# Output weights by head group through a DRAM scratch, an epsilon column, whole-bank gate products and earlier transposes in a linear-attention and gated-MLP block

## The chip, the cores and the metric

The kernel runs on one core of one Trainium2 chip. The metric is the device time of one execution in microseconds (us); the median of three runs of the kernel before is 190.47 us (190.45 to 190.97). A core has a matrix engine (PE, whose weight loads the profile lists as PEld), a vector engine (DVE), a scalar engine (ACT), a GpSimd engine (POOL) and a sync engine (SP). Each works through its own list of instructions in order and waits for the others on semaphores. In this kernel SP and ACT issue the DMAs; the profile calls SP's queue q1 and ACT's q10. ps is the PE's result memory, eight banks of 512 f32 per partition.

## The reference

Two stages, 2048 tokens, width 448, 16 heads of 28, hidden width 1792; inputs and output are bf16.

```python
qkv = (x @ wqkv).reshape(B, S, 3, H, Dh)          # x is layer-normed
phi = lambda t: jnp.where(t > 0, t + 1, jnp.exp(t)) + 1e-6
pq, pk = phi(q), phi(k)
kv = jnp.einsum("bhsd,bhse->bhde", pk, v)
z = jnp.einsum("bhsd->bhd", pk)
num = jnp.einsum("bhqd,bhde->bhqe", pq, kv)
den = jnp.einsum("bhqd,bhd->bhq", pq, z)[..., None] + 1e-6
h = x + (num / den).reshape(B, S, D) @ wo
# then, on layernorm(h):
h2 = h + (_gelu(h_n @ w_gate) * (h_n @ w_up)) @ w_down
```

## The kernel before

The tokens are 16 tiles of 128 (t = 0 to 15) and 8 pairs of tiles (p = 0 to 7). Everything stays on the chip between the load of x and the store of the result.

**Keys and queries.** Each tile is normalized, transposed and multiplied by the key or query weights, four matmuls of 448 columns into one of ps banks 0 to 3 (tasks `k_t`, `q_t`, function `proj`, L469). ACT reads a query bank twice, `eq_t` (exp, L496) and `rq_t` (relu, L497), and only then is the bank free for the query tile four places later. Key tiles add to sums in banks 4 to 7 (`pt`, L488). So the v projection is never made per token: when all key tiles are in, the sums are copied to SBUF (`evpA`, `evpD`, L516 to L521), multiplied by wv into the per-head matrix kv (`kv`, L527), masked to its diagonal blocks (`kvm`, L531), and multiplied by wo to the output weights w2 (`w2_c`, L547), seven matmuls because the 448 rows are cut in 128-row pieces and the head groups are 112 rows wide. w2 is copied out of ps (`evwA`, `evwD`), and two DMAs (`dws0`, `dws1`, on SP's queue) make a copy w2s with the two halves of the partitions exchanged.

**Attention output of a pair** (`a2_pair`). pq is finished (`cq`, `aq`), multiplied by z (`t1`), summed per head (`dr`, L572 or L586), 1e-6 is added on ACT (`deA`, `deP`, L574 and L588), inverted (`rd`) and multiplied in (`pn`, into pqn). Pair 0 is transposed on the PE (`tro`); pairs 1 to 7 by a DMA on SP's queue (`oT_p`, L605). The product with w2 is 4 matmuls per tile for pair 0 (`out1_t`, L617), and for the others 14 matmuls of 64 rows, two at a time on the two halves of the array, in two parts (`outA_p`, `outB_p`, L627 and L628), of which B waits for A's results. Then follow the residual (`hr`), the second layer norm and the transpose of hn, on the PE for pair 0 (`trh`, L654), by DMA for the rest (`hT`).

**MLP.** Gate and up products go to the two halves of the array, into two alternating gate banks (0, 1) and up banks (6, 7) (`gu`, L731 and L733). ACT applies gelu (`ge`, L751), DVE multiplies by the up product (`hm`, L753), both in halves of 256 columns. The first four tiles are worked two at a time (14 units `gu2_0` to `gu2_13` of two hidden blocks), the rest four at a time (`gu4`). The down product is L697 and, for the last two tiles, L678.

**Order.** The tasks are recorded in program order, each with the buffers it reads and writes. The table ORDERS then gives for each engine the order of its tasks as a list of task numbers, and the semaphore waits are derived from the buffers. HOLD names for some tasks which of several waits comes first. The MLP weights are loaded by SP behind the DMA transposes of the x tiles, four loads of 672 KB (first 768 hidden columns) and 896 KB (the rest), gate and up each into 64 partitions; the last is the up load of 896 KB.

Of the kernel before, what the change touches and what calls it, by code (L numbers as in the profile page):

```python
# [822 lines left out]
```

## Time and profile before

| what | value |
|---|---|
| median of 3 runs | 190.47 us |
| profiled execution, first to last instruction | 188.3 us |
| PE busy | 184.3 us (98%) |
| PEld busy | 109.2 us (58%) |
| DVE busy | 129.3 us (69%) |
| ACT busy | 76.5 us (41%) |
| POOL busy | 50.0 us (27%) |
| granted PE clock | 1.000 over the whole span |
| DMA | 17.11 MB, of it 16.32 MB on q1 and 0.52 MB on q10 |

The span is 2.2 us shorter than the median of the runs; what lies around it (launch and end) is taken as unchanged. A line of a timeline is: start, duration, engine, source line, operation, what is written from what, how many, and in brackets the engine's idle time before it. Durations of neighbours overlap, since an engine starts the next instruction before the last has left its pipeline; the step from start to start is what counts. Durations of matmuls are modelled ends.

### The profile page before, as it was taken

Reading aid. Unit: us, or ns where it says so; the run is one execution under the profiler, and the core shown is the slowest. Engines: PE = TensorE matmul, PEld = TensorE weight load, DVE = VectorE, ACT = ScalarE, POOL = GpSimd, SP = SyncE. Lnnn points to the kernel's source line nnn. Section 1 sums busy time; section 2 is a strip of 40 time slices with the busy share of each in tenths; the row PEclk is TensorE's granted clock in tenths of the full one; section 3 lists DMA queues with packets and bytes.
Section 4 is the critical chain, followed back from the end, with each engine's and each line's share of the span. In section 5 each row is a group of like instructions: output and inputs, shape, how many; then the busy total and the mean of one; then the engine's idle time right before and its main releaser. Section 6 shows DMA issues by size and latency. Waiting matters only on the chain.

```text
span 188.3 us, 4459 instructions
## 1 busy us (share of the span) xinstructions
PE 184.3 (98%) x1813; PEld 109.2 (58%) x1813; DVE 129.3 (69%) x330; ACT 76.5 (41%) x220; POOL 50.0 (27%) x91
## 2 busy tenths in 40 slices
PE   7999999999999999999999999999999999999994
PEld 7545555555688788965554555555545545454554
DVE  4999959999899998786796762562645244335432
ACT  3878752799963231432234222321242222224100
POOL 6067910704505686033614000206100000000000
PEclk9999999999999999999999999999999999999999
DMA  5996458999393526820005720000096000002024
GB/s 169 387 231 88 96 104 194 218 222 174 65 320 64 95 52 116 84 52 0 0 3 98 144 54 0 0 3 2 3 135 111 3 0 24 3 0 98 3 79 140
DMA packets 35076, 17.11 MB, mean 91 GB/s; under 512 B 26864, under 2 KB 33648, under 8 KB 35056
## 3 DMA queue, kind: packets, MB, share of 16 engines
q1 hardware_dynamic: 34432, 16.32, 41.1%
q10 hardware_dynamic: 624, 0.52, 0.8%
q8 instruction: 14, 0.23, 0.5%
q14 instruction: 6, 0.05, 0.1%
HBM read 8.26 MB, written 1.84 MB: 54 GB/s over the span
## 4 chain that ended last, share of the span: by engine, by line
PE 94%; DVE 3%; DMA 1%; issue 0%
PE ps L733 38%; PE ps L697 19%; PE ps L469 12%; PE ps L731 9%; PE ps L488 6%; PE ps L627 3%; PE ps L678 3%; PE ps L628 2%; DMA x_sb<-in_A_x_dram 1%; DVE st L413 1%; PE ps L617 1%; PE ps L547 1%; PE ps L527 1%; PE ps L443 0%; PE ps L654 0%; DVE den L572 0%
## 5 line engine op out<-in xcount | busy, mean ns | idle before, releaser
L733 PE MATMUL ps<-hnT,wgu_sb 64*128 64x512 bf16 (+1 forms) x490 | 88.8, 333 | 0.0
L731 PE MATMUL ps<-hnT,wgu_sb 64*128 64x512 bf16 (+1 forms) x490 | 88.6, 333 | 0.0
L751 ACT ACTIVATE gl<-ps 128x256 bf16<-128x256 f32 x112 | 36.6, 383 | 85.3 <-PE ps L731 84.4
L753 DVE TENSOR_TENSOR hh<-ps,gl 128x256 bf16<-128x256 f32 x112 | 42.1, 416 | 41.4 <-ACT gl L751 41.3
L733 PEld LDWEIGHTS ps<-hnT,wgu_sb 64*128 64x128 bf16 x490 | 45.2, 94 | 32.9 <-DVE hh L753 3.4
L731 PEld LDWEIGHTS ps<-hnT,wgu_sb 64*128 64x128 bf16 x490 | 45.4, 94 | 2.5
L697 PE MATMUL ps<-wd_sb,hh 64*128 64x448 bf16 x392 | 41.5, 349 | 0.0
L697 PEld LDWEIGHTS ps<-wd_sb,hh 64*128 64x128 bf16 x392 | 23.2, 94 | 14.5
L469 PE MATMUL ps<-wqk_sb,xnT 128*128 128x448 bf16 x128 | 27.4, 353 | 0.0
L413 DVE BATCH_NORM_STATS2 st<-x_sb 128x6 f32<-128x448 bf16 x32 | 19.2, 612 | 1.8 <-DMA x_sb<-in_A_x_dram 1.7
L585 POOL TENSOR_TENSOR t<-pq,zbc 128x448 f32<-128x448 bf16 x12 | 12.3, 1042 | 23.7 <-DVE pq L583 22.0
L469 PEld LDWEIGHTS ps<-wqk_sb,xnT 128*128 128x128 bf16 x128 | 11.9, 98 | 11.4 <-DVE pk L482 0.8
L488 PE MATMUL ps<-pk,xnn 128*128 128x448 bf16 x64 | 13.9, 352 | 0.0
L627 PE MATMUL ps<-w,pqnT 64*128 64x448 bf16 x49 | 11.5, 349 | 0.1
L425 POOL TENSOR_SCALAR ln<-mv 128x2 f32<-128x2 f32 x7 | 2.0, 291 | 35.2 <-DVE mv L414 35.0
L480 ACT ACTIVATE e<-ps 128x448 bf16<-128x448 f32 x16 | 8.5, 539 | 5.6 <-PE ps L469 5.5
L628 PE MATMUL ps<-pt_sb,pqnT 64*128 64x448 bf16 x42 | 10.2, 350 | 0.0
L633 DVE TENSOR_TENSOR x_sb<-ps,x_sb 128x448 bf16<-128x448 f32 x16 | 9.6, 616 | 0.7 <-PE ps L628 0.6
L662 POOL TENSOR_SCALAR hn<-x_sb,nm,rs 128x448 bf16<-128x448 bf16 x14 | 9.9, 719 | 0.4
L482 DVE SCALAR_TENSOR_TENSOR pk<-ps,e 128x448 bf16<-128x448 f32 x16 | 9.8, 617 | 0.1
L488 PEld LDWEIGHTS ps<-pk,xnn 128*128 128x128 bf16 x64 | 6.3, 98 | 5.9 <-DVE pk L482 0.3
L453 POOL TENSOR_SCALAR xnn<-x_sb,nm,rs 128x448 bf16<-128x448 bf16 x12 | 8.9, 744 | 2.2 <-ACT rs L422 1.9
(85 smaller groups left out, 160.5 us busy)
## 6 DMA issues: line engine op xcount, KB each, us to landing
out_dram<-x_sb SPq DMA_DIRECT2D x15, 112.0 KB, 1.8
wd_sb<-in_B_w_down_dram SPq DMA_DIRECT2D x1, 1568.0 KB, 8.4
x_sb<-in_A_x_dram SPq DMA_DIRECT2D x3, 448.0 KB, 5.9
wgu_sb<-in_B_w_gate_dram SPq DMA_DIRECT2D x1, 896.0 KB, 12.1
wgu_sb<-in_B_w_up_dram SPq DMA_DIRECT2D x1, 896.0 KB, 16.5
wgu_sb<-in_B_w_gate_dram SPq DMA_DIRECT2D x1, 672.0 KB, 6.1
wgu_sb<-in_B_w_up_dram SPq DMA_DIRECT2D x1, 672.0 KB, 8.5
wo_sb<-in_A_wo_dram SPq DMA_DIRECT2D x1, 392.0 KB, 7.5
```

The source lines that it names most:

```text
L413: op("dve", lambda e: e.bn_stats(st[:, t, :], src_ap), [b_src], [b_st[t]], "bnst%s_%d" % (tag, t))
L469: ins = e.matmul(ps[:, bk, 0:D], xnT[:, t, k, :], wqk_sb[:, k, c0:c0 + D], start=(k == 0), stop=(k == 3))
L488: ins = e.matmul(ps[:, BK_PT[c], 0:D], xnn[:, t % XN_R, c * 128:(c + 1) * 128], pk[:, ip, :], start=(t == 0), stop=(t == T - 1))
L585: op("pool", lambda e, n=n: e.tensor_tensor(t1[:, n, :], pq[:, a + n, :], zbc[:, :], ALU.mult), [b_pq[a + n]] + b_z, [b_t1[n]], "t1p_%d" % ...
L627: e.matmul(ps[:, BK_OUT[0], 0:D], pqnT[ra, i2, sg // 2, :], w2[ra, sg // 2, :], start=(sg == 0), stop=(sg == 5))
L628: ins = e.matmul(ps[:, BK_OUT[1], 0:D], pqnT[rb, i2, 3 + (sg + 1) // 2, :], (w2 if sg == 6 else w2s)[rb, sg // 2, :], start=(sg == 0), sto ...
L662: op("pool", lambda e, t=t, sh=sh: e.tensor_scalar(hn[:, sh, 0:D], x_sb[:, t, :], nm2[:, t:t + 1], rs2[:, t:t + 1], ALU.add, ALU.mult), [b ...
L697: ins = e.matmul(ps[:, bko[half][n], 0:D], hh[rows, j, sl[n]], wd_sb[rows, j, :], start=(j == 0 and (half == 0 or p == 6)), stop=(j == NJ ...
L731: first = e.matmul(psG[:, jj * N:(jj + 1) * N], wgu_sb[A_, k, j * 128:(j + 1) * 128], hnT[A_, ka_, c0:c0 + N], start=(k == 0), stop=(k == ...
L733: ins = e.matmul(psU[:, jj * N:(jj + 1) * N], wgu_sb[B_, k, j * 128:(j + 1) * 128], hnT[B_, kb_, c0:c0 + N], start=(k == 0), stop=(k == NK ...
L751: G.add("act", lambda e, gi=gi, cs_=cs_, psG=psG: e.activation(gl[:, gi, cs_], psG[:, cs_], AF.Gelu_apprx_tanh), r=[b_ps[BK_G[i]]], w=[b_g ...
L753: op("dve", lambda e, dst=dst, srcU=srcU, srcL=srcL: e.tensor_tensor(dst, srcU, srcL, ALU.mult), [b_ps[BK_U[i]], b_glh], [b_ar[j_][t % HR] ...
```

## The change

- **w2 by head group.** The masked kv has no padding any more. Four matmuls, one for each group of 112 rows, give w2g (112 partitions, 4 groups). The memset of the padding and the copy `kvd` go.
- **Repacking through DRAM.** For the paired products of pairs 2 to 7, w2g is written to a DRAM scratch (`dw2w`) and read back twice (`dw2r0`, `dw2r1`) as w2p, seven pieces of 64 rows on both halves of the partitions. All three are issued by ACT and stand in ACT's order; each read waits for the write. `dws0` and `dws1` go. w2p takes the memory of pt_sb and wv_sb.
- **Pair 1** is multiplied like pair 0, with w2g, four matmuls per tile (`out1_2`, `out1_3`); its DMA transpose has eight blocks in place of seven.
- **Epsilon column.** t1 has a 29th column per head that holds 1e-6, so the sum over 29 includes it; the ten ACT instructions `deA` and `deP` go.
- **Whole bank.** For `gu2` units, gelu and product take 512 columns at once (`geW`, `hmW`): 14 each in place of 28.
- **Transposes.** Of the seven `trh` transposes, only the last waits for the copy `wr64`.
- **Orders.** All five lists and HOLD are new.

```diff
@@ ORDERS, HOLD
-    "29 35 37 44 46 66 53 55 71 76 62 64 79 84 70 89 75 83 104 99 88 114 119 129 103 153 118 141 133 177 165 145"
...
-    66: (36,), 141: (140,), 165: (164,), 214: (213,), 216: (215,), 323: (302,), 326: (324,), 431: (340,), 704:
...
+    20: (19,), 32: (31,), 34: (33,), 35: (34,), 37: (34,), 41: (40,), 43: (42,), 44: (43,), 46: (43,),
...
@@ buffers
+        pt_sb, wv_sb, w2p = pv_sb[:, 0:4, :], pv_sb[:, 4:8, :], pv_sb[:, 0:NK, :]
+        w2g = sb("w2g", [GW, NG, D], BF16)
+        w2d = nc.dram_tensor("w2_bounce", [D, D], BF16)
+        t1 = sb("t1", [128, 2, H, DH + 1], F32)
+        op("pool", lambda e: e.memset(t1[:, :, :, DH:DH + 1], EPS), [], [b_epsd], "epsd")
-        op("pool", lambda e: e.memset(kvz[:, GW:15 * GW], 0.0), [], [b_kvm], "kvzpad")
@@ w2
-                gs = (c, c + 1) if c < 3 else (3,)
-                    ins = e.matmul(ps[:, BK_W2[c], 0:D], kvc(g, c), wo_sb[:, g, :], start=(g == gs[0]), stop=(g == gs[-1]))
+        for g in range(NG):
+            G.add("pe", lambda e, g=g: e.matmul(ps[0:GW, BK_W2[g], 0:D], kvz[:, g * GW:(g + 1) * GW], wo_sb[:, g, :], start=True, stop=True),
+                  r=[b_kvm, b_wo], w=[b_ps[BK_W2[g]]], name="w2_%d" % g)
...
-            dma("sp", w2s[to, :, :], w2[of, 0:3, :], [b_w2s[h]], "dws%d" % h, r=b_w2[0:3], after=xts[-1:])
+        dma("act", w2d.ap().rearrange("(g p) n -> p g n", p=GW), w2g[:, :, :], [b_w2d], "dw2w", r=b_w2)
+        for h, rows in enumerate((A_, B_)):
+            dma("act", w2p[rows, :, :], w2d.ap().rearrange("(k p) n -> p k n", p=64), [b_w2p[h]], "dw2r%d" % h, r=[b_w2d])
@@ a2_pair
-                    op("act", lambda e, i=i: e.activation(den[:, i, :], den[:, i, :], AF.Identity, bias=eps_d[:, 0:1]), [b_den[i], b_epsd], [b_den[i]], "deA_%d" % t)
-                op("act", lambda e: e.activation(den[:, i:i + 2, :], den[:, i:i + 2, :], AF.Identity, bias=eps_d[:, 0:1]), b_den[i:i + 2] + [b_epsd], b_den[i:i + 2], "deP_%d" % p)
...
-            if p == 0:
+            if p < 2:
                 for n in range(2):
                     def fout(e, W, n=n):
                         ins = None
                         for g in range(NG):
                             W(g)
-                            ins = e.matmul(ps[:, BK_OUT[n], 0:D], pqnT[:, i2, 4 * n + g, :], w2[:, g, :], start=(g == 0), stop=(g == NG - 1))
+                            ins = e.matmul(ps[:, BK_OUT[n], 0:D], pqnT[0:GW, i2, 4 * n + g, :], w2g[:, g, :], start=(g == 0), stop=(g == NG - 1))
...
-                    parts.append(G.add("pe", foutp, r=b_pqnT[i2] + b_w2 + b_w2s, w=[b_ps[b_] for b_ in BK_OUT], name="out%s_%d" % (part, p), sync=parts[-1:]))
+                    parts.append(G.add("pe", foutp, r=b_pqnT[i2] + b_w2p, w=[b_ps[b_] for b_ in BK_OUT], name="out%s_%d" % (part, p), sync=parts[-1:]))
...
+                        for m, k in enumerate((0, 1, 2, 4, 5, 6, 3)):
+                            W(m)
@@ gu_chunk
-                for hh_ in range(2):
-                    cs_ = slice(hh_ * 256, (hh_ + 1) * 256)
+                for hh_ in range(2 if nj == 1 else 1):
+                    cs_ = slice(hh_ * 256, (hh_ + 1) * 256) if nj == 1 else slice(0, 512)
```

ACT while the w2 copies and the query tiles run. Before, `w<-ps` are the copies of w2 and `pqnT<-ps` those of the transposes `tro`:

```order
L551 ACTIVATE w<-ps 128x448 x2
L497 ACTIVATE pq<-ps 128x448
L602 ACTIVATE pqnT<-ps 128x512 x2
L497 ACTIVATE pq<-ps 128x448
L496 ACTIVATE eq<-ps 128x448
L497 ACTIVATE pq<-ps 128x448
L496 ACTIVATE eq<-ps 128x448 x3
```

Now two of the three DMAs stand in this stretch, w_bounce being the DRAM scratch and pv_sb the memory of w2p:

```order
L610 ACTIVATE w2g<-ps 112x448 x2
L567 ACTIVATE eq<-ps 128x448
L417 DMA w_bounce<-w2g 112x4x448
L567 ACTIVATE eq<-ps 128x448
L660 ACTIVATE pqnT<-ps 128x512
L568 ACTIVATE pq<-ps 128x448 x2
L660 ACTIVATE pqnT<-ps 128x512
L567 ACTIVATE eq<-ps 128x448 x2
L568 ACTIVATE pq<-ps 128x448 x2
L567 ACTIVATE eq<-ps 128x448
L491 ACTIVATE ln<-mv,eps_t 128x1
L417 DMA pv_sb<-w_bounce 64x7x448
```

The write stands behind `eq_7`. Between it and the first read stand ten activations (`eq_6`, `evo_0`, `rq_6`, `rq_8`, `evo_1`, `eq_9`, `eq_8`, `rq_9`, `rq_11`, `eq_11`) and `ln2_0`; behind the first read follow `eq_10`, `rstd2_0`, `rq_10`, `ln2_1`, `rstd2_1` and the second read.

PE from the last query tiles ahead of kv to the first product of pair 1, before:

```order
L469 MATMUL ps<-wqk_sb,xnT 128x448 x8
L527 MATMUL ps<-pt_sb,wv_sb 112x112 x16
L469 MATMUL ps<-wqk_sb,xnT 128x448 x8
L547 MATMUL ps<-wo_sb,hh 128x448 x6
L469 MATMUL ps<-wqk_sb,xnT 128x448 x4
L547 MATMUL ps<-wo_sb,hh 128x448
L599 MATMUL ps<-ident,pqn 128x128 x8
L469 MATMUL ps<-wqk_sb,xnT 128x448 x4
L617 MATMUL ps<-w,pqnT 128x448 x8
L469 MATMUL ps<-wqk_sb,xnT 128x448 x24
L654 MATMUL ps<-ident,hn 128x128 x14
```

and now, from kv on (L598 is kv, L607 w2, L657 `tro`, L675 `out1`):

```order
L598 MATMUL ps<-pv_sb 112x112 x16
L540 MATMUL ps<-wqk_sb,xnT 128x448 x4
L607 MATMUL ps<-wo_sb,hh 112x448 x4
L540 MATMUL ps<-wqk_sb,xnT 128x448 x4
L657 MATMUL ps<-ident,pqn 128x128 x4
L540 MATMUL ps<-wqk_sb,xnT 128x448 x8
L657 MATMUL ps<-ident,pqn 128x128 x4
L675 MATMUL ps<-w2g,pqnT 128x448 x4
L540 MATMUL ps<-wqk_sb,xnT 128x448 x4
L675 MATMUL ps<-w2g,pqnT 128x448 x4
L540 MATMUL ps<-wqk_sb,xnT 128x448 x20
L713 MATMUL ps<-ident,hn 128x128 x14
```

One query tile in place of two stands between kv and w2. The last query tiles are `q_12`, `q_10`, `q_13`, `q_15`, `q_14`, and `q_14` goes into the bank that `q_10` leaves. Behind the last row `out1_2` and `out1_3` (8 matmuls) take the place of `outA_1` and `outB_1`; `outB_2` now follows `outA_2` directly, where two MLP units stood between them.

DVE around the masking of kv, before (L521 copies the last key sum, `evpD_2`; L531 is `kvm`):

```order
L569 TENSOR_TENSOR t<-pq,zbc 128x448
L572 TENSOR_REDUCE den<-t 128x16
L521 CAST pt_sb<-ps 128x448
L575 RECIPROCAL rd<-den 128x16
L572 TENSOR_REDUCE den<-t 128x16 x2
L531 TENSOR_TENSOR hh<-ps,mask 112x4x112
```

and now (L592 is `evpD_2`, L602 `kvm`, L635 `pn_0`):

```order
L628 TENSOR_TENSOR t<-pq,zbc 128x16x28
L592 CAST pv_sb<-ps 128x448
L631 TENSOR_REDUCE den<-t 128x16
L633 RECIPROCAL rd<-den 128x16
L631 TENSOR_REDUCE den<-t 128x16
L635 TENSOR_TENSOR pqn<-pq,rd 128x4x112
L602 TENSOR_TENSOR hh<-ps,mask 112x448
```

`evpD_2` moved ahead of `dr_0`, and `pn_0` ahead of `kvm`.

More of the change, by code (lines that the diff above doesn't have):

```diff
@@ L258, in bass_sequential_preLN__linear_attn_block__glu_gated_geglu__prompt_kernel @@
         wqk_sb = sb("wqk_sb", [128, 4, 2 * D], BF16)
-        wv_sb = sb("wv_sb", [128, 4, D], BF16)
+        pv_sb = sb("pv_sb", [128, 8, D], BF16)
+        pt_sb, wv_sb, w2p = pv_sb[:, 0:4, :], pv_sb[:, 4:8, :], pv_sb[:, 0:NK, :]
         wo_sb = sb("wo_sb", [GW, NG, D], BF16)
@@ L297, in bass_sequential_preLN__linear_attn_block__glu_gated_geglu__prompt_kernel @@
         gl = sb("gl", [128, 3, 512], BF16)
-        kvz = hh[0:GW, 6:9, :].rearrange("p a b -> p (a b)")
-        w2s = pt_sb[:, 0:3, :]
+        t1f = t1[:].rearrange("p n h d -> p n (h d)")[:, :, 0:D]
+        kvz = hh[0:GW, 6, 0:D]
         ps = es.enter_context(nc.psum_tensor("ps", [128, 8, 512], F32))
@@ L392, in bass_sequential_preLN__linear_attn_block__glu_gated_geglu__prompt_kernel @@
         op("pool", lambda e: e.memset(pt_sb[:, 3, :], 0.0), [], [b_pt[3]], "ptpad")
-        op("pool", lambda e: e.memset(pqn[:, 0, :].rearrange("p (n c) -> p n c", n=2)[:, :, D:512], 0.0), [], b_pqn[0], "pqnpad")
-        op("pool", lambda e: e.memset(kvz[:, GW:15 * GW], 0.0), [], [b_kvm], "kvzpad")
+        for i_ in range(2):
+            op("pool", lambda e, i_=i_: e.memset(pqn[:, i_, :].rearrange("p (n g c) -> p n g c", n=2, g=NG)[:, :, :, GW:128], 0.0), [], b_pqn[i_], "pqnpad_%d" % i_)
         tbl1 = G.add("act", lambda e: e.preload_act_table_set("natural_log_exp_and_others"), name="tbl1", kind="nosync", after=[tx1])
@@ L554, in bass_sequential_preLN__linear_attn_block__glu_gated_geglu__prompt_kernel @@
-        for h, (to, of) in enumerate(((A_, B_), (B_, A_))):
-            dma("sp", w2s[to, :, :], w2[of, 0:3, :], [b_w2s[h]], "dws%d" % h, r=b_w2[0:3], after=xts[-1:])
+           [b_ps[BK_KV], b_mask], [b_kvm], "kvm")
+        for g in range(NG):
+            G.add("pe", lambda e, g=g: e.matmul(ps[0:GW, BK_W2[g], 0:D], kvz[:, g * GW:(g + 1) * GW], wo_sb[:, g, :], start=True, stop=True),
+                  r=[b_kvm, b_wo], w=[b_ps[BK_W2[g]]], name="w2_%d" % g)
+            if g % 2 == 0:
+                op("act", lambda e, g=g: e.activation(w2g[:, g, :], ps[0:GW, BK_W2[g], 0:D], AF.Identity), [b_ps[BK_W2[g]]], [b_w2[g]], "evwA_%d" % g)
+            else:
+                op("dve", lambda e, g=g: e.tensor_copy(w2g[:, g, :], ps[0:GW, BK_W2[g], 0:D]), [b_ps[BK_W2[g]]], [b_w2[g]], "evwD_%d" % g)
@@ L604, in a2_pair @@
             else:
-                G.add("sp", lambda e, i2=i2: e.dma_start_transpose(pqnT[:, i2, 0:NK, :], pqn[:, i2, 0:2 * D]),
+                G.add("sp", lambda e, i2=i2: e.dma_start_transpose(pqnT[:, i2, 0:8 if p == 1 else NK, :], pqn[:, i2, 0:1024 if p == 1 else 2 * D]),
                       r=b_pqn[i2], w=b_pqnT[i2], name="oT_%d" % p, kind="dma")
@@ L744, in gu_chunk @@
                         th = tiles
-                        njh = nj // 2
+                        njh = nj
                         jr = list(range(j0 + hh_ * njh, j0 + (hh_ + 1) * njh))
```

65 lines of the change are left out of this document (21 added, 44 removed), and 132 rows, old and new, of tables (HOLD, ORDERS).

## Prediction

> **What bounds the kernel now.** I read the page's busy shares and its chain of waits first, then the timelines of PE, ACT and DVE between the last key tile and the first MLP unit, where the change does its work, and last the DMA views of that stretch.
>
> ```profile
> PE 184.3 (98%) x1813; PEld 109.2 (58%) x1813; DVE 129.3 (69%) x330; ACT 76.5 (41%) x220; POOL 50.0 (27%) x91
> PE 94%; DVE 3%; DMA 1%; issue 0%
> ```
>
> PE is busy for 98% of the span and makes 94% of the chain. From the first query tile to the last down product it is the only thing that counts: time goes down where PE gets less work or one of its few gaps closes, and up wherever something new makes it wait. The PE timeline around the change:
>
> ```profile
> 34.23 1.68 PE L469 MATMUL ps<-wqk_sb,xnT 128*128 128x448 bf16 x8
> 35.96 1.03 PE L527 MATMUL ps<-pt_sb,wv_sb 128*112 128x112 bf16 x16
> 36.83 1.68 PE L469 MATMUL ps<-wqk_sb,xnT 128*128 128x448 bf16 x8
> 38.34 1.30 PE L547 MATMUL ps<-wo_sb,hh 112*128 112x448 bf16 x6
> 43.15 4.70 PE L469 MATMUL ps<-wqk_sb,xnT 128*128 128x448 bf16 x24
> 47.69 0.94 PE L654 MATMUL ps<-ident,hn 128*128 128x128 bf16 x14
> 49.15 0.35 PE L628 MATMUL ps<-w,pqnT 64*128 64x448 bf16 x1
> 49.56 0.36 PE L627 MATMUL ps<-w,pqnT 64*128 64x448 bf16 x1
> ```
>
> 24 query matmuls start at 43.15 and the next group at 47.69: 4.54/24 = 0.189 us each. Eight from 34.23 end their starts at 35.74, and kv starts at 35.96: a gap of 0.22. From the last product of `outA_1` (49.15) to the first of `outB_1` (49.56) is 0.41 instead of 0.19, again 0.22, because part B waits for part A's results. These are the only two gaps in the stretch. In the chain of waits the product of pair 1 and the first MLP unit begin at
>
> ```profile
> 48.63 0.29 PE ps L627
> ...
> 50.30 0.11 PE ps L733
> ```
>
> **The change part by part.** *Copy of the last key sum.* kv waits for `evpD_2`, which DVE does behind `dr_0`.
>
> ```profile
> 34.10 0.62 DVE L569 TENSOR_TENSOR t<-pq,zbc 128x448 f32<-128x448 bf16 x1
> 34.76 0.62 DVE L572 TENSOR_REDUCE den<-t 128x16 f32<-128x448 f32 x1
> 35.29 0.61 DVE L521 CAST pt_sb<-ps 128x448 bf16<-128x448 f32 x1
> 37.19 0.61 DVE L531 TENSOR_TENSOR hh<-ps,mask 112x448 bf16<-112x448 f32 x1
> 38.62 0.56 DVE L576 TENSOR_TENSOR pqn<-pq,rd 128x448 bf16<-128x448 bf16 x1
> ```
>
> Moved ahead of `dr_0` it ends at about 35.3, so kv starts at 35.75: -0.21. What is late next is `kvm`. From 34.7 DVE does `evpD_2`, `dr_0`, `rd_0`, `dr_1`, `pn_0` (steps of about 0.53, 0.65, 0.16, 0.55, 0.47), so `kvm` starts near 37.05 and ends near 37.7; PE is through kv and one query tile at 35.75 + 1.03 + 0.76 = 37.54. Price: +0.15 (bounds 0 to +0.3).
>
> *w2.* Four matmuls in place of seven: 3 x 0.189 = -0.57. Matmuls of 112 rows cost what those of 128 do here (L547 steps as L469).
>
> *Pair 1.* `outA_1` and `outB_1` take 50.30 - 48.63 = 1.67 (seven steps and the gap); `out1_2` and `out1_3` take 8 x 0.189 = 1.51: -0.16. But `outB_2` now stands directly behind `outA_2`, where two units covered the same wait: +0.22.
>
> *Cover.* The epsilon instructions, the removed copy `kvd`, the whole-bank gelu and product, and the one-column-longer sums lie on ACT and DVE beside a busy PE: 0 as long as no PE task waits for them. The nearest is `gu2_2`, whose up bank is freed by the first product.
>
> ```profile
> 51.12 1.28 ACT L762 ACT_TABLE_LOAD   x1
> 52.41 0.66 ACT L751 ACTIVATE gl<-ps 128x256 bf16<-128x256 f32 x2
> 53.10 0.76 DVE L753 TENSOR_TENSOR hh<-ps,gl 128x256 bf16<-128x256 f32 x2
> ```
>
> That product ends at 53.86, and PE reaches `gu2_2` at 53.95, so the cover is 0.1. ACT loses five epsilon steps of about 0.21 before the table load and gains three DMA issues of about 0.55 (rows below), 0.6 more; the whole-bank pair of gelu and product gives back about 0.2, and `outB_2`, now ahead of `gu2_2`, 0.8. I take 0 (bounds 0 to +0.4). `trh` no longer waits for `wr64`, but nothing waited there: 0. Columns of t1 at a stride of 29 on POOL and DVE have no row; a change there of a tenth of their time would still lie beside PE, so 0.
>
> Without the DMAs: -0.21 + 0.15 - 0.57 - 0.16 + 0.22 = **-0.57** (bounds -0.8 to -0.2). In a walk through the new order, q_14 then starts at 46.46 and the first MLP unit at 49.5, against 50.30 in the chain before.
>
> *The repacking.* The old pair of DMAs went through SP's queue behind the MLP weights:
>
> ```profile
> 28.65 0.63 SPq L346 DMA_DIRECT2D wgu_sb<-in_B_w_gate_dram  x1
> 29.33 0.76 SPq L346 DMA_DIRECT2D wgu_sb<-in_B_w_up_dram  x1
> DMA to landing us min/median/max: 12.1/14.3/16.5
> 40.37 1.16 SPq L346 DMA_DIRECT2D pt_sb<-w  x2
> pt_sb<-w SPq DMA_DIRECT2D x2, 168.0 KB, 5.7
> 40.00:46.00 6.00, 6.00 (x40) 3.29 (x38) 6.00 (x13) 5.84 (x16) 2.04 (x2) 1.00 1.18 209
> ```
>
> (The third row is of the two 896 KB loads above it.) The last load lands at 29.33 + 16.5 = 45.8, and the DMA engines are full until then (share 1.18 between 40 and 46). The two copies landed 5.7 us after their issues at 40.4 and 40.9, at 46.1 to 46.6, and nothing needed them before 48.6.
>
> Now ACT issues the write of 392 KB once `evwD_3` is done. From the walk: `kvm` to 37.7, w2 to 38.45, both copies on DVE to 39.3, so the write leaves at about 39.5. ACT then does ten activations and `ln2_0`.
>
> ```profile
> 42.28 0.56 ACT L496 ACTIVATE eq<-ps 128x448 bf16<-128x448 f32 x1
> 42.70 0.57 ACT L497 ACTIVATE pq<-ps 128x448 bf16<-128x448 f32 x1
> 45.39 0.49 ACT L420 ACTIVATE ln<-mv,eps_t 128x1 f32<-128x1 f32 x2
> 45.77 0.35 ACT L422 ACTIVATE rs<-ln 128x1 f32<-128x1 f32 x2
> L346 ACTq DMA_DIRECT2D wqk_sb<-in_A_wqkv_dram x2: 457/490/523, 1.2 to 1.7; - x2
> ```
>
> Ten steps of 0.42 to 0.48 and one of 0.19 make 4.55. An issue on ACT took 0.49; I take 0.55, since the larger loads on SP took 0.63. ACT stands at the first read at 39.5 + 0.55 + 4.55 = 44.6, and **there it waits for the write to land**. Behind it on ACT stand `eq_10` and `rq_10`, which free the bank of `q_14`; with `rstd2_0` between them they take 0.55 + 0.42 + 0.11 + 0.54 = 1.62 from the end of the wait. PE wants `q_14` at 46.46, so a write that lands after 44.8 stalls PE by the excess: the write has 5.3 us.
>
> When does it land? Lower bound: as ACT's 336 KB load at the start, 4.2 us, at 43.7; no stall. Upper bound: 1.5 us behind the last MLP load, at 47.3. What decides is whose turn it is on the engines. The start of the kernel shows both queues loaded at once, in two windows of 0.4 us (4.1 to 4.5, and 5.0 to 5.4):
>
> ```profile
> 1.25 1.01 ACTq L346 DMA_DIRECT2D wqk_sb<-in_A_wqkv_dram  x2
> 1.71 0.43 SPq L346 DMA_DIRECT2D wqk_sb<-in_A_wqkv_dram  x1
> wqk_sb<-in_A_wqkv_dram ACTq DMA_DIRECT2D x1, 336.0 KB, 4.2
> wqk_sb<-in_A_wqkv_dram ACTq DMA_DIRECT2D x1, 56.0 KB, 5.0
> q10 hardware_dynamic: 167, 0.15, 106.5%
> q1 hardware_dynamic: 5, 0.00, 2.2%
> q1 hardware_dynamic: 170, 0.15, 108.4%
> q10 hardware_dynamic: 3, 0.00, 1.4%
> ```
>
> In the first window ACT's 336 KB load has nearly all packets, though SP's load issued at 1.71 is waiting; in the second SP has them, while ACT's 56 KB, issued at about 1.7, land only at 6.7. The queues do not share packet by packet: the engines finish one queue's transfer and then turn to the other's. The load before the last MLP load landed at 28.65 + 12.1 = 40.7, so the last one has the engines from about 40 on; 896 KB at 209 GB/s are 4.4 us of them. A write that leaves at 39.5 and needs part of a microsecond to reach the engines misses the change of turn and comes behind it, as the old copies did. I take their landing, **46.3**: the stall is 46.3 - 44.8 = **+1.5**.
>
> The Trainium skill speaks of this in "DMA: Bandwidth & Descriptors", section "Queues, rings and completion order": an engine goes round its queues packet by packet, a packet being some 9 to 17 descriptors and at most 64. The trace agrees on the turns, with the 167 packets against 5 above, but shows none that ends inside a transfer. By that rule the time would be that of the second rival, 190.1, instead of 191.4.
>
> Once it has landed, reads of 392 KB each leave at 46.3 and 48.3 and land by about 52, ahead of `outA_2` at 54. The DMA transpose of pair 1, issued at 43.1 behind the same load, has until 49.4.
>
> Sum against the profiled span: 188.3 - 0.57 + 1.5 = 189.2, and with the 2.2 us by which the median of the runs stands above that span, **191.4 us** (190.47 + 0.93).
>
> **The rivals.**
>
> 1. *The write lands in time* (by 44.8), because ACT's queue gets a turn between the two 896 KB loads or writes to DRAM overtake loads into SBUF. For it: 336 KB in 4.2 us on this queue at the start. Against it: the two windows. Then only the -0.57 is left: 189.9. This is the one on the other side, and the landing of one transfer decides: 44.8 against 46.3.
> 2. *Short turns.* If a turn is half of the 896 KB load (2.1 us at the 209 GB/s of the row), the write gets two turns, near 41.8 and 44.3, and lands near 45.0: stall 0.2, 190.1. The windows speak against it, though with smaller rows than those of the MLP loads.
> 3. *The reads are late as well.* If the second read comes behind the 1568 KB load of w_down, issued at about 50 and 8.4 us to landing, `outA_2` waits a further 1 to 2 us: 192.9.
>
> ```profile
> wd_sb<-in_B_w_down_dram SPq DMA_DIRECT2D x1, 1568.0 KB, 8.4
> ```
>
> **How the numbers follow.** The forecast has a chance of 0.44 (its own range 190.9 to 192.3, from landings between 45.8 and 47.3), rival 1 0.36, rival 2 0.12, rival 3 0.08. The range 189.6 to 192.3 takes in rival 1 with its bound of -0.8 and the forecast's upper bound. A change under 0.3% (0.57 us) can hardly be told from none: rival 1 lies on that line, so I give faster 0.22 (rival 1 and a little of its better side), same 0.27 (the rest of it, rival 2 and the forecast's lowest edge), slower 0.51.
>
> **What would show it.** In the changed profile: kv starting at 35.75; four L607 matmuls in a row after one query tile; `out1_2` without a gap; an ACT wait at the first read (DMA of w_bounce, landing 6 to 7 us after its issue), and behind it PE idle of 1 to 2 us ahead of the last query tile. If the write lands within 5.3 us and PE shows no gap, the forecast is wrong and rival 1 right; a gap at `outA_2` released by a DMA would be rival 3, one at `gu2_2` released by DVE a mistake in the cover.

## The result, and the profile after

The changed kernel takes 191.72 us (median of 6 runs, 191.35 to 191.98), the kernel before beside it 190.75 (6 runs, 190.45 to 190.97): a ratio of 1.0049, with a 95% interval of 1.0034 to 1.0064. The forecast was 191.4, its range 189.6 to 192.3. The profiled execution took 191.98 us, the slowest of the six, with a span of 190.2; all that follows in this section is of that execution. A few executions of the kernels below took over 1.5% longer than the fastest of the same kernel; the ratios leave them out, the medians and ranges do not.

From the page: the span, the busy shares, and the chain of waits by engine.

```profile
span 190.2 us, 4399 instructions
...
PE 184.5 (97%) x1804; PEld 113.2 (60%) x1804; DVE 128.7 (68%) x315; ACT 73.3 (39%) x196; POOL 50.0 (26%) x91
...
PE 85%; DMA 7%; DVE 5%; SPq 1%; ACT 1%; ACTq 0%; issue 0%
```

PE has nine matmul records fewer and the same busy time, yet its part of the chain fell from 94 to 85%: DMA has 7% and DVE 5% where they had 1% and 3%. So the time is lost in waits and not in work. The timeline of PE (start, length, line, shapes, count; in brackets the idle time before and what ended it) shows where:

```profile
34.61 1.68 PE L540 MATMUL ps<-wqk_sb,xnT 128*128 128x448 bf16 x8
36.12 0.99 PE L598 MATMUL ps<-pv_sb 128*112 128x112 bf16 x16
36.95 0.92 PE L540 MATMUL ps<-wqk_sb,xnT 128*128 128x448 bf16 x4
38.37 0.96 PE L607 MATMUL ps<-wo_sb,hh 112*112 112x448 bf16 x4 [0.51 <-DVE hh L602]
...
44.17 3.19 PE L540 MATMUL ps<-wqk_sb,xnT 128*128 128x448 bf16 x16
48.66 0.93 PE L540 MATMUL ps<-wqk_sb,xnT 128*128 128x448 bf16 x4 [1.30 <-ACT pq L568]
...
50.20 1.68 PE L675 MATMUL ps<-w2g,pqnT 112*128 112x448 bf16 x8
51.82 0.28 PE L790 MATMUL ps<-hnT,wgu_sb 64*128 64x256 bf16 x1
...
55.45 0.35 PE L685 MATMUL ps<-pv_sb,pqnT 64*128 64x448 bf16 x1
...
55.87 0.36 PE L685 MATMUL ps<-pv_sb,pqnT 64*128 64x448 bf16 x1
```

Query matmuls step by 0.189 us. Eight from 34.61 end at 36.12, where kv (L598) starts: its gap is gone. Four from 36.95 end at 37.71, and w2 (L607) starts at 38.37: a new gap of **0.67**. Sixteen from 44.17 end at 47.20, and the four of `q_14` start at 48.66: a gap of **1.46**. `outA_2` to `outB_2` is 55.45 to 55.87, a step of 0.41 and so a gap of 0.22. At 54.9, ahead of `outA_2`, and at 56.45, where `gu2_2` begins, there is none.

The gap at `q_14` goes back from PE to ACT, and from ACT to a DMA. The timeline of ACT:

```profile
40.18 0.36 ACTq L417 DMA_DIRECT2D w_bounce<-w2g  x1
...
45.49 0.29 ACT L491 ACTIVATE ln<-mv,eps_t 128x1 f32<-128x1 f32 x1 [0.33 <-DVE mv L485]
46.85 0.64 ACTq L417 DMA_DIRECT2D pv_sb<-w_bounce  x1
47.53 0.54 ACT L567 ACTIVATE eq<-ps 128x448 bf16<-128x448 f32 x1 [1.75 <-PE ps L540]
```

ACT has finished `ln2_0` at 45.78 and issues the first read only at 46.85. The row names PE as what ended the 1.75 us of idle time, but PE had been done with that tile long before; the time runs out with the landing of the write, 40.18 + 6.6 = 46.8. Both are in the DMA view (the median time from issue to landing), with the packets of the two queues in the windows from 42 to 43 and from 44 to 45 us (packets, MB, share of 16 engines; q1 is SP's queue, q10 ACT's):

```profile
w_bounce<-w2g ACTq DMA_DIRECT2D x1, 392.0 KB, 6.6
wgu_sb<-in_B_w_up_dram SPq DMA_DIRECT2D x1, 896.0 KB, 16.1
...
q1 hardware_dynamic: 100, 0.20, 101.5%
...
q10 hardware_dynamic: 335, 0.30, 96.1%
q1 hardware_dynamic: 14, 0.02, 9.7%
```

Two microseconds after the write is issued, the engines still serve nothing but SP's queue; two microseconds later they serve the write, and it lands 1.1 us behind the load that SP issued at 29.6 (29.6 + 16.1 = 45.7).

### The profile page after: what moved, and what is told of

It is laid out like the page before. It is cut to its first block, busy times and chain, and to the rows that moved or that the text cites. A ratio compares the mean times of both kernels' runs of the same rounds, so it can differ in the third digit from the quotient of the medians.

```text
span 190.2 us, 4399 instructions
## 1 busy us (share of the span) xinstructions
PE 184.5 (97%) x1804; PEld 113.2 (60%) x1804; DVE 128.7 (68%) x315; ACT 73.3 (39%) x196; POOL 50.0 (26%) x91
## 3 DMA queue, kind: packets, MB, share of 16 engines
q10 hardware_dynamic: 2016, 1.72, 3.2%
## 4 chain that ended last, share of the span: by engine, by line
PE 85%; DMA 7%; DVE 5%; SPq 1%; ACT 1%; ACTq 0%; issue 0%
PE ps L792 40%; PE ps L756 19%; PE ps L540 7%; PE ps L790 6%; PE ps L559 5%; DMA w_bounce<-w2g 3%; DMA x_sb<-in_A_x_dram 3%; PE ps L737 3%; PE ps L685 2%; PE ps L686 2%; DVE den L631 1%; PE ps L675 1%; SPq L417 1%; DVE w2g L612 1%; DVE st L484 1%; DVE pqn L635 0%
## 5 line engine op out<-in xcount | busy, mean ns | idle before, releaser
L810 ACT ACTIVATE gl<-ps 128x256 bf16<-128x256 f32 (+1 forms) x98 | 35.3, 414 | 87.1 <-PE ps L790 86.2
L812 DVE TENSOR_TENSOR hh<-ps,gl 128x256 bf16<-128x256 f32 (+1 forms) x98 | 41.1, 456 | 40.7 <-ACT gl L810 40.7
L790 PEld LDWEIGHTS ps<-hnT,wgu_sb 64*128 64x128 bf16 x490 | 45.2, 94 | 2.9 <-ACT eq L567 0.4
L756 PEld LDWEIGHTS ps<-wd_sb,hh 64*128 64x128 bf16 x392 | 25.4, 94 | 12.2
L540 PE MATMUL ps<-wqk_sb,xnT 128*128 128x448 bf16 x128 | 27.9, 353 | 1.5 <-ACT pq L568 1.3
L644 POOL TENSOR_TENSOR t<-pq,zbc 128x448 f32<-128x448 bf16 x12 | 12.9, 1093 | 27.2 <-DVE pq L642 27.2
L721 POOL TENSOR_SCALAR hn<-x_sb,nm,rs 128x448 bf16<-128x448 bf16 x14 | 10.9, 784 | 0.5
L685 PE MATMUL ps<-pv_sb,pqnT 64*128 64x448 bf16 x42 | 9.9, 349 | 0.1
L686 PE MATMUL ps<-pv_sb,pqnT 64*128 64x448 bf16 x42 | 9.9, 349 | 0.0
L567 ACT ACTIVATE eq<-ps 128x448 bf16<-128x448 f32 x16 | 8.6, 566 | 2.1 <-PE ps L540 1.7
## 6 DMA issues: line engine op xcount, KB each, us to landing
wgu_sb<-in_B_w_up_dram SPq DMA_DIRECT2D x1, 896.0 KB, 16.1
```

The source lines that it names most:

```text
L540: ins = e.matmul(ps[:, bk, 0:D], xnT[:, t, k, :], wqk_sb[:, k, c0:c0 + D], start=(k == 0), stop=(k == 3))
L644: op("pool", lambda e, n=n: e.tensor_tensor(t1[:, n, :, 0:DH], pq[:, a + n, :].rearrange("p (h d) -> p h d", h=H), zbc[:, :].rearrange("p ...
L685: e.matmul(ps[:, BK_OUT[0], 0:D], pqnT[ra, i2, sg // 2, :], w2p[ra, sg, :], start=(sg == 0), stop=(sg == 5))
L686: ins = e.matmul(ps[:, BK_OUT[1], 0:D], pqnT[rb, i2, 3 + (sg + 1) // 2, :], w2p[rb, sg, :], start=(sg == 0), stop=(sg == 5))
L721: op("pool", lambda e, t=t, sh=sh: e.tensor_scalar(hn[:, sh, 0:D], x_sb[:, t, :], nm2[:, t:t + 1], rs2[:, t:t + 1], ALU.add, ALU.mult), [b ...
L756: ins = e.matmul(ps[:, bko[half][n], 0:D], hh[rows, j, sl[n]], wd_sb[rows, j, :], start=(j == 0 and (half == 0 or p == 6)), stop=(j == NJ ...
```

## The experiments

Each kernel is the changed one with the edit shown. Ratios are to the kernel before on the same chip (for the numbered kernels 190.5 to 190.7 us, 11 to 17 runs). Waits of PE are worked out from the steps of its matmuls.

| Kernel | us | ratio to before | write issued, landed | PE waits that matter |
|---|---|---|---|---|
| the change | 191.72 | 1.0049 | 40.2, 46.8 | 1.46 at q_14, 0.67 at w2 |
| 1 reads by SP | 190.65 | 1.0003 | 39.9, 46.7 | 0.41 at outA_2, 0.67 at w2 |
| 2 last load behind oT_1 | 196.21 | 1.0285 | 40.1, 43.2 | 3.4 at outA_2 |
| 3 last load in four | 192.15 | 1.0080 | 40.2, 46.8 | 1.44 at q_14 |
| 4 pn_0 behind kvm | 191.63 | 1.0050 | 39.9, 46.6 | 1.72 at q_14, 0.12 at w2 |
| 5 last load behind the write | 191.95 | 1.0067 | 40.4, 43.5 | 1.70 at out1_2 |
| 6 = 5 with pn_0 | 191.83 | 1.0060 | 39.8, 43.2 | 1.33 at out1_2 |
| 7 = 6, outB_2 later | 192.99 | 1.0118 | 39.9, 42.9 | 1.4 at out1_2, 1.4 at gu2_4 |
| 8 no DMAs, pn_0 | 190.45 | 0.9990 | none | 0.23 at trh_0 |
| 9 loads spread | 196.69 | 1.0282 | 40.4, 43.4 | 1.6 at gu2_3, 2.3 at gu2_7 |
| 10 = 9 with pn_0 | 196.30 | 1.0278 | 40.6, 43.7 | 1.8 at gu2_3, 3.3 at gu2_7 |
| 11 = 10, small waits | 195.95 | 1.0248 | 40.0, 43.2 | 0.6 at gu2_2, 0.8 at gu2_3, 2.9 at gu2_7 |
| 12 part of the load behind the write, pn_0 | 190.43 | 1.0004 | 39.9, 45.0 | 0.31 at q_14 |

### The first four: is it ACT's wait, and why is the write late?

**1. SP issues the two reads**, behind `oT_1`, so that ACT waits for no DMA.

```diff
-            dma("act", w2p[rows, :, :], ... "dw2r%d" % h, r=[b_w2d])
+            dma("sp", w2p[rows, :, :], ... "dw2r%d" % h, r=[b_w2d])
```

> Both reads of the scratch are issued by SP, behind the transpose of pair 1, instead of ACT; all else as changed. Theory (ACT's wait for the landing of the write holds eq_10 and rq_10, and these q_14): the write still lands near 46.8, but ACT does not wait for it, the gap of 1.46 us ahead of the last query tile goes, and the time is 191.7 - 1.4 = 190.3 us. Rival (ACT is late because of its own work and DMA issues): only the two issues of 0.6 us go, part of the gap stays, 191.1 us or more. If the reads now come too late, a gap appears at outA_2 instead.

190.65 us (190.18 to 191.25, 12 runs), ratio 0.9990 to 1.0016. The write landed as late as before, and the gap at `q_14` is gone: the stall came from ACT standing at the read. 1.07 us came back (0.9 by the ratios) rather than all of it, because `oT_2`, issued behind the second read, is now late for `outA_2`. On the timeline of PE:

```profile
53.56 0.35 PE L680 MATMUL ps<-pv_sb,pqnT 64*128 64x448 bf16 x1 [0.25 <-DMA pqnT<-pqn]
```

**2. The last MLP load is issued behind `oT_1`**, at 45.5 instead of 29.6. SP's order alone is changed:

```diff
- ... dwu0 dwg1 dwu1 oT_1 oT_2 dwd oT_3 ...
+ ... dwu0 dwg1 oT_1 dwu1 oT_2 dwd oT_3 ...
```

> Only SP's order is changed: the last MLP load (896 KB, up) is issued behind the transpose of pair 1, so no large load is in front of the write. Theory (the write waits for the turn of that load): it lands 2.5 to 4 us after its issue instead of 6.6, ACT does not wait at the first read, 190.3 us; the load lands by 51, before its first use at 55. Rival (a write of this form to DRAM takes 6.6 us by itself): the landing and the gap stay, 191.7 us.

The write landed 3.2 us after its issue, and `q_14` waited only 0.1. But 196.21 us (195.32 to 196.85): the load now lies between the first read and everything behind it. The DMA view and then the timeline of PE:

```profile
w_bounce<-w2g ACTq DMA_DIRECT2D x1, 392.0 KB, 3.2
```

```profile
56.87 0.53 PE L680 MATMUL ps<-pv_sb,pqnT 64*128 64x448 bf16 x1 [3.29 <-DMA pqnT<-pqn]
```

That the write came in time shows that the load is what delays it. It does not yet tell by what rule. (The wait is only part of the 5.6 us above the kernel before: from 57 to 61 us, behind it, the granted clock was 0.63; see the last section.)

**3. The last load is cut into four transfers**, issued at the same time. If the engines changed queues after a whole transfer, ACT's write would now get its turn behind one of the pieces.

```diff
- wgu_sb[B_, :, cs], B_w_up[:, cs]                        # one transfer, 896 KB
+ wgu_sb[B_, k0:k1, cs], B_w_up[64 * k0:64 * k1, cs]      # k0:k1 = 0:2, 2:4, 4:6, 6:7
```

> The last MLP load is cut in four transfers (8, 8, 8 and 4 rows for each DMA engine), at the same place in SP's order and with the same bytes. Theory (a queue keeps the engines until its transfer is through, then the other queue has its turn): the write gets its turn at the next border and lands near 44 instead of 46.8; no or little wait on ACT, 190.3 to 190.6 us. Rival (the write is behind all bytes that SP has queued, wherever their borders are): it lands at 46.8 as before, 191.7 us.

192.15 us (191.89 to 192.51). Four issues from 29.65 on the timeline of SP, and in the DMA view the same 6.6 us for the write:

```profile
29.65 2.68 SPq L413 DMA_DIRECT2D wgu_sb<-in_B_w_up_dram  x4
```

```profile
w_bounce<-w2g ACTq DMA_DIRECT2D x1, 392.0 KB, 6.6
```

The write landed behind all four. **The turn by whole transfers, on which the prediction rested, falls.** What fits all three runs is simpler: both queues are served in the order of issue, whatever the borders of the transfers. I took this as the theory for the rest.

**4. On DVE, `pn_0` stands behind `kvm`**, so that w2 does not wait for it.

```diff
- ... rd_0 dr_1 pn_0 kvm rd_1 ...
+ ... rd_0 dr_1 kvm pn_0 rd_1 ...
```

> On DVE, pn_0 stands behind kvm instead of ahead of it; all else as changed. The gap of 0.67 us ahead of the first w2 matmul shrinks to about 0.1 and the write leaves 0.5 us earlier. Theory (the landing of the write is set by the end of the last MLP load, not by its issue): it still lands near 46.8, the gap ahead of q_14 grows by what the other one loses, and the time stays at 191.7 us. Rival (the landing is a fixed 6.6 us behind the issue): all moves 0.5 us forward, 191.2 us.

191.63 us (191.44 to 191.80): the w2 gap fell from 0.67 to 0.12, and the gap at `q_14` grew from 1.46 to 1.72, since PE comes 0.5 us earlier to a wait whose end is set by the load. (The load itself landed 0.2 earlier here, at 45.4, and the write with it. So this run alone would also fit a write of a fixed 6.6 us; runs 2, 5 and 12 do not.) On the timeline of PE:

```profile
48.41 0.93 PE L535 MATMUL ps<-wqk_sb,xnT 128*128 128x448 bf16 x4 [1.56 <-ACT pq L563]
```

### Order of issue, tested in both directions

**5. The last load goes out just behind the write**, ahead of `oT_1`.

```diff
+            if i == 1:
+                G.dep(G.all[-1], [t for t in G.all if t.name == "eq_6"])   # eq_6 follows dw2w on ACT
```

> The last 896 KB MLP load (the up half, second group) is issued by SP only when ScalarE has left eq_6, the instruction right behind its write of the packed weights (about 41.2 us instead of 29.6), and ahead of oT_1; nothing else differs from the change. Theory A (the 16 engines serve what both queues hand them in the order of issue, over queues): the write is now ahead of that load and behind the first half's load, which landed at 41.1, so it lands near 43.3 instead of 46.8, ScalarE reads without waiting, the 1.46 us gap at q_14 falls to under 0.2, the load lands at about 47 to 47.5 and oT_1 behind it at about 48 to 48.5, just ahead of its reader at 48.7: 190.2 to 190.6 us. Theory B (the engines share their time between the two queues by packets or bytes, and the write takes its 6.6 us because it always gets a part only): the write would be slowed by the load again and land at 45 or later, gap at q_14 0.3 to 1.4 us, 190.6 to 191.7 us. Theory C (the write is slow by itself, by its 448-column rows): it lands at 46.8 as before, 191.7 us; the 3.2 us that it took when the load came 5 us behind it speaks against this.

The write landed 3.1 us after its issue and ACT read without a wait, as the order of issue has it. The time was missed: 191.95 us (191.67 to 194.6). The load took 8.4 us, not the 5.8 to 6.3 I allowed, and `oT_1`, issued 3.2 us behind it, landed behind it. The DMA view, then the timeline of PE:

```profile
wgu_sb<-in_B_w_up_dram SPq DMA_DIRECT2D x1, 896.0 KB, 8.4
w_bounce<-w2g ACTq DMA_DIRECT2D x1, 392.0 KB, 3.1
...
pqnT<-pqn SPq DMA_TRANSPOSE x1, 6.2
```

```profile
50.81 0.93 PE L672 MATMUL ps<-w2g,pqnT 112*128 112x448 bf16 x4 [1.54 <-DMA pqnT<-pqn]
```

The stall of one queue became the stall of the other, and of a like size.

**6 and 7. With `pn_0` behind `kvm` (6), and with `outB_2` behind `gu2_3` as well (7).**

```diff
- ... outA_2 outB_2 gu2_2 gu2_3 ...
+ ... outA_2 gu2_2 gu2_3 outB_2 ...
```

> As the run before, and on VectorE the normalization pn_0 of tile 0 stands behind kvm, so that the head-group products w2 don't wait for it. Theory A: the gap ahead of w2 falls from 0.67 to 0.12 us, the write goes out 0.3 us earlier, and now nothing takes the gain back, since the landing no longer hangs on the end of the last load: 0.4 to 0.55 us below the run before, 189.7 to 190.1 us, faster than the kernel before by 0.3 to 0.5%. Rival: tro_0, which reads pn_0, comes late and gives the gain back: as the run before.

> As the run before, and on TensorE the second half of pair 2's output product (outB_2) stands behind gu2_3 instead of directly behind outA_2, whose accumulation it continues: the 0.22 us between the two halves is covered by gu2_3's matmuls. Theory: 0.2 us less than the run before, 189.5 to 189.9 us. Rival: the residual, LayerNorm and transposes of tiles 4 and 5 come later by gu2_3's length and a gate product further on waits for them: 0.3 to 1 us more than the run before.

Both missed. 6 took 191.83 us (191.52 to 192.02): `out1_2` still waits 1.33 us for `oT_1`. 7 took 192.99 (192.86 to 196.33), in the way of its rival and a little more than its 0.3 to 1 us: `hr_4` stands ahead of `hmW0_2` on DVE and waits for `outB_2`, and a gate unit waits for that product. From the waits of PE in run 7:

```profile
PE ps L789 <- DVE hh L809: 1.2, 1, 1.2
```

So moving `outB_2` there costs more than the 0.22 us that it was to save.

### The change without its DMAs

**8. The write and both reads are left out**, with `pn_0` as in 4.

```diff
-        dma("act", w2d.ap()..., "dw2w", r=b_w2)
-            dma("act", w2p[rows, :, :], ..., "dw2r%d" % h, r=[b_w2d])
```

> The write to DRAM and the two reads back are left out (the packed products of pairs 2 to 7 then multiply by the value weights that lie in that tile, so the output is not the reference's), with pn_0 behind kvm as above. It measures what the change is worth with its DMAs taken away: the forecast's sum without the stall was -0.57, of which the w2 wait is mended here: 189.7 to 190.1 us, and no gap at q_14. If the three DMAs cost something beside the stall (ScalarE's three issues of 0.36 to 0.64 us, transfers behind them that land later), this run lies below the run with the late load and pn_0 by that much; theory A expects a difference under 0.2 us.

190.45 us (190.15 to 191.03, 12 runs), ratio 0.9977 to 1.0003. There is no gap over 0.05 us at `q_14`, but the time is 0.3 to 0.7 us above what I expected. On the timeline of PE:

```profile
37.62 0.96 PE L602 MATMUL ps<-wo_sb,hh 112*112 112x448 bf16 x4
38.42 0.92 PE L535 MATMUL ps<-wqk_sb,xnT 128*128 128x448 bf16 x4
39.34 0.40 PE L649 MATMUL ps<-ident,pqn 128*128 128x128 bf16 x4
...
43.77 3.76 PE L535 MATMUL ps<-wqk_sb,xnT 128*128 128x448 bf16 x19
47.60 1.01 PE L705 MATMUL ps<-ident,hn 128*128 128x128 bf16 x14
48.45 1.68 PE L667 MATMUL ps<-w2g,pqnT 112*128 112x448 bf16 x8
```

Four query matmuls from 38.42 end at 39.18, and `tro_0` starts at 39.34: 0.16. Nineteen from 43.77 end at 47.37, and `trh_0` starts at 47.60: 0.23. Where PE reaches the next thing sooner, a small wait on DVE's results stands there. (The first of the two comes with the move of `pn_0`: in the changed kernel `tro_0` follows at once.) So the rest of the change is worth little: 0.26 us below the kernel before beside it, with an interval that reaches from 0.44 below to 0.06 above. The 0.57 that the first rival had for a write in time lies outside it.

### Can the order be mended?

**9 to 11. The last load behind `oT_2`, and w_down behind `oT_3`** (9); with `pn_0` behind `kvm` (10); with `outB_2` behind `gu2_2`, `hr_4` behind `hmW0_2`, `tro_0` behind `q_9` (11).

```diff
- ... dwg1 dwu1 oT_1 oT_2 dwd oT_3 hT_3 hT_2 ...
+ ... dwg1 oT_1 oT_2 dwu1 oT_3 dwd hT_3 hT_2 ...
```

> Only the order of SyncE's issues differs from the change: the last 896 KB MLP load goes out behind oT_2 (about 50.3 us instead of 29.6; its first reader is gu2_6 at about 61), and the w_down load behind oT_3 (about 57.6 instead of 52; its first reader is downA_0 at about 67), so that nothing large is issued between the write of the packed weights and the two transposes that pairs 1 and 2 wait for. Theory A (service in order of issue over both queues): the write lands about 3.2 us after its issue, near 43.4, the reads near 48 and 50, oT_1 near 47.5, oT_2 near 51.5, the load near 55.5 and w_down near 66; no gap over 0.3 us at q_14, out1_2, outA_2, gu2_6 or downA_0. What is left is the run without the three DMAs (190.45 us) with the w2 gap of 0.67 instead of 0.12 us: 190.8 to 191.2 us. Theory B (the two loads had hidden something else, or a load issued late is late for its reader): a gap of 1 us or more at gu2_6, outA_3 or downA_0, 191.5 us or more.

> As the run before, with pn_0 behind kvm on VectorE. Theory A: the DMAs now cost nothing, so the time is that of the run without them, 190.45 us (190.2 to 190.8), 0.3 to 0.6 below the run before. Rival: the three DMAs cost time beside the stall as well (ScalarE's issues, shared engines): 191 us or more.

> As the run before, and three moves that take the small waits left: outB_2 behind gu2_2 on TensorE with hr_4 behind hmW0_2 on VectorE (the 0.22 us between outA_2 and outB_2), and tro_0 behind q_9 on TensorE (0.15 us of waiting for pn_0). If both waits are covered and none is new: 0.2 to 0.4 us less than the run before, 189.9 to 190.4 us, ahead of the kernel before by 0.2 to 0.4%. Rival: the residual of tile 4, later by one gate unit, makes a later gate unit wait as in the run with outB_2 behind gu2_3 (1.38 us there, 0.3 to 1.4 us here): 190.7 to 191.8 us.

196.69 (194.55 to 198.33), 196.30 (194.31 to 197.85) and 195.95 us (194.66 to 198.87): all missed by over 5 us, in the way of the first one's theory B, though at other places than it named. The write landed 3.0 to 3.2 us after its issue, `out1_2` and `outA_2` did not wait, and `q_14` waited 0.1 to 0.3. But I had taken the first readers too late. `gu2_3` reads the last load at 57.0, and it lands at 51.1 + 7.7 = 58.8; `gu2_7` reads `hT_3` and `hT_2` at 66, and they land behind w_down near 69. From the waits of PE in run 10:

```profile
PE ps L785 <- DMA hnT<-hn: 3.2, 1, 3.2
PE ps L787 <- DVE hn L718: 1.6, 1, 1.6
```

(The second row blames DVE; the gap ends with the landing of the load.) The time of run 11 was not decided by its three moves, but its trace shows that they gain nothing: `tro_0` no longer waits, and `out1_0` behind it waits 0.2 instead; with `outB_2` behind `gu2_2` the 0.22 is gone, and PE waits 0.6 within `gu2_2` for a product of DVE.

**12. Three of the last load's seven row blocks go out behind the write**, the first four as before, with `pn_0` behind `kvm`. It differs from run 3 in the time of issue of a part, not only in the cut.

```diff
- wgu_sb[B_, :, cs], B_w_up[:, cs]                        # issued at 29.6
+ wgu_sb[B_, 0:4, cs], B_w_up[0:256, cs]                  # issued at 29.5
+ wgu_sb[B_, 4:7, cs], B_w_up[256:448, cs]                # issued behind eq_6, at 40.9
```

> The last MLP load is cut in two: its first four row blocks of seven (512 KB) go out at 29.6 us as before, the last three (384 KB) behind the write of the packed weights (issued when ScalarE has left eq_6, near 41 us), ahead of oT_1; and pn_0 stands behind kvm. Theory A (service in order of issue): the first part lands near 43.7 to 44.6, the write 1.2 us behind it, 44.9 to 45.8, against ScalarE's first read at 45.1; the rest lands near 47 to 47.6 and oT_1 near 48 to 48.5, against its reader at 48.4. Gaps at q_14 0.1 to 0.7, at out1_2 0 to 0.3: 190.4 to 191.0 us, about the kernel before and the run without the three DMAs, 0.8 to 1.3 us below the change with pn_0 moved. Theory B (the engines share by packets or bytes): as with the load cut in four at one time, the write lands near 46.6 and the gap stays at 1.4 us or more: 191.6 us.

190.43 us (190.26 to 191.86, 12 runs), ratio 0.9989 to 1.0020, the expected time. ACT has the first read out at 45.2, without a wait, and `out1_2` (L674) follows the transposes at once. The DMA view, the timeline of ACT and that of PE:

```profile
wgu_sb<-in_B_w_up_dram SPq DMA_DIRECT2D x1, 512.0 KB, 13.4
w_bounce<-w2g ACTq DMA_DIRECT2D x1, 392.0 KB, 5.1
wgu_sb<-in_B_w_up_dram SPq DMA_DIRECT2D x1, 384.0 KB, 5.3
```

```profile
45.20 0.29 ACT L487 ACTIVATE ln<-mv,eps_t 128x1 f32<-128x1 f32 x1 [0.33 <-DVE mv L481]
45.21 0.63 ACTq L413 DMA_DIRECT2D pv_sb<-w_bounce  x1
```

```profile
47.01 0.93 PE L536 MATMUL ps<-wqk_sb,xnT 128*128 128x448 bf16 x4 [0.15 <-ACT pq L564]
47.77 0.94 PE L712 MATMUL ps<-ident,hn 128*128 128x128 bf16 x14
48.55 1.68 PE L674 MATMUL ps<-w2g,pqnT 112*128 112x448 bf16 x8
```

The first part landed at 29.5 + 13.4 = 42.9. Behind it waited the write (issued at 39.9) and SP's second part (40.9), and the write landed first: 45.0 against 46.1. That speaks against a rival which the runs before leave open, that SP's queue simply goes ahead of ACT's.

The 0.31 us left at `q_14` is no landing. It stands in runs 6, 7, 10 and 11 too, all with `pn_0` moved, so that PE reaches `q_14` earlier. Run 8, with `pn_0` moved and no DMAs, has none: ACT runs `eq_10` at 45.3 there, and at 45.9 here, where it issues DMAs in between.

Of the edits tried, this one and the first bring the changed kernel back to the time of the kernel before; none beats that by a measurable amount.

## Why the prediction came out, and what in it was wrong

| Step of the prediction | forecast | profiled |
|---|---|---|
| kv no longer waits | -0.21 | -0.22 |
| w2 waits for kvm | +0.15 | +0.67 |
| four w2 matmuls for seven | -0.57 | -0.57 by count |
| pair 1 as pair 0 | -0.16 | -0.05 |
| outB_2 directly behind outA_2 | +0.22 | +0.22 |
| q_14 waits for ACT, ACT for the write | +1.5 | +1.46 |
| a later start | none | +0.38 |
| sum | +0.93 | +1.89 |

The spans of the two profiled executions differ by 1.9 us, as the last column has it, the medians of the runs by 0.97. Two things lie between. PE reaches kv 0.38 us later in this execution (36.12, against 35.96 less its gap of 0.22). That varies from one execution to the next: in the twelve kernels with an edit, which do the same work up to there, kv starts between 35.8 and 36.6, and the spans of the changed kernel's six runs go from 189.6 to 190.2. And the time beside the span fell by about 0.25: 2.0 us in the median of the runs of the kernel before, 1.75 in the kernels with the change, except run 3 with its three more transfers (2.0). I have no cause for that; it stays open.

**Right: the place, the chain and the size of the stall.** The write was issued at 40.2 (forecast 39.5) and landed at 46.8 (46.3); ACT stood at the first read, and PE waited 1.46 us (1.5) at `q_14`. Runs 1, 2 and 12 take ACT's wait away in three ways, and the gap falls to 0.0, 0.1 and 0.3. That nothing else would be late held too: there is no gap at `outA_2` or `gu2_2` in the changed kernel. That 1.5 came out as a size owes something to luck: the landing was 0.5 later than forecast, and PE came to `q_14` 0.7 later (47.2 against 46.46).

**Wrong: the step "the engines finish one queue's transfer and then turn to the other's".** It gave the right landing for the wrong reason. Run 3 contradicts it; the runs bear out service in the order of issue: 3.0 to 3.4 us when the load was issued behind the write (runs 2, 5 to 7, 9 to 11), 5.1 when four sevenths were ahead of it (run 12), 6.6 to 6.8 when all of it was, in one piece or in four. The prediction's own evidence says the same: at the start ACT's 336 KB, issued at 1.25, came first, then SP's load of 1.71, then ACT's 56 KB of 1.75 (they landed at 5.4, 6.5 and 6.8). In the trace of the kernel before, 154 pairs of transfers were in flight together, 25 of them with one on each queue, and not one landed against its order of issue; the same holds for the 164 pairs (32 across queues) of the changed kernel. The order is not strict, though: in all 14 traces 4 of 2277 pairs landed the other way round (runs 5, 8, 10 and 12), each across the two queues, at the start of the kernel and issued within 0.05 us of each other. Counted that way, the landing could have been read from the first trace without any rule on turns. What the runs do not show is by what means the engines keep that order.

The Trainium skill says in "DMA: Bandwidth & Descriptors", section "Queues, rings and completion order", that an engine goes round its queues by packets, and also that the signal of completion lands only after every earlier write of that engine, over its queues. The second fits the landings here. The first does not show: in the window from 42 to 43 us, with the write waiting for 2 us, ACT's queue has no packet. With it falls the second rival (short turns, 190.1 us; half of the load at 209 GB/s is 2.2 us there and not 2.1, which changes nothing).

**Mis-sized: the w2 wait and pair 1.** "Price: +0.15" for w2 was 0.67. Two terms make the difference. "35.75 + 1.03 + 0.76" takes kv at the modelled length of its row. Its step to the next matmul, which counts, was 0.87 in the kernel before (35.96 to 36.83) and 0.83 in the changed one (36.12 to 36.95), so PE came to w2 0.2 us sooner. And `kvm` came 0.3 later: the order of the steps on DVE was as I had it, but `pn_0` took 0.90 us, where the same operation had 0.56. The timeline of DVE:

```profile
36.38 0.58 DVE L631 TENSOR_REDUCE den<-t 128x16 f32<-128x464 f32 x1
36.88 0.90 DVE L635 TENSOR_TENSOR pqn<-pq,rd 128x448 bf16<-128x448 bf16 x1
37.71 0.61 DVE L602 TENSOR_TENSOR hh<-ps,mask 112x448 bf16<-112x448 f32 x1
```

It starts while POOL computes t1 of the next tiles (from 36.26). Moved behind `kvm` (run 4), it took 0.61, though POOL was at work there too; POOL's two products beside it took 2.94 us then, and 2.42 in the changed kernel. The Trainium skill, "Trainium Architecture — The Big Picture", section "What this means for kernel authors", says that VectorE and GpSimd share a pair of ports to on-chip memory that one of them holds exclusively. A wait for that port, now on one engine and now on the other, would fit these times, but no run here separates it.

The other term is pair 1. I set 8 x 0.189 = 1.51 against the 1.67 from the chain. The timeline of PE in the kernel before has

```profile
47.69 0.94 PE L654 MATMUL ps<-ident,hn 128*128 128x128 bf16 x14
48.57 0.36 PE L627 MATMUL ps<-w,pqnT 64*128 64x448 bf16 x1
...
50.14 0.27 PE L733 MATMUL ps<-hnT,wgu_sb 64*128 64x256 bf16 x1
```

Fourteen transposes take 14 x 0.056 = 0.78 us, as in the changed kernel (49.42 to 50.20), and so end at 48.47. From there to the first MLP unit it is 1.67, as I had it, though the chain's rows at 48.63 and 50.30 are not these two points. The changed piece takes 51.82 - 50.20 = 1.62. In both, the step from the last matmul on the whole array to the first on its halves is 0.10 longer than the others: 48.57 stands 0.10 behind 48.47, and 51.82 as far behind 50.20 + 1.51. My 1.51 left that out.

Run 8 lays open two small waits (0.16 at `tro_0`, 0.23 at `trh_0`) that were not in the sum. So "without the DMAs: -0.57" was too good by 0.3 us (190.45 against the 190.71 of the kernel before beside it) in the runs' times, and by 0.5 in the median spans (188.65 against 188.7).

That 191.4 lies so near 191.72 is in part luck. The terms of the sum were too low by 0.6 (0.5 for w2, 0.1 for pair 1). Against that stand two things that were not in the sum: the 0.25 beside the span, and that the two profiled executions lie farther apart than the medians. The one of the kernel before, at 188.3, was 0.2 to 0.5 us shorter than that kernel's median spans in the later runs (188.5 to 188.8), and the one of the changed kernel, at 190.2, was 0.25 longer than its median of 189.95. Taken together they bring the 1.89 of the last column down to 0.9 to 1.2, where 0.97 was measured.
